# A smaller tile of zeros, a ninth product of zeros at the start, and one product fewer in two later waits

## The chip, the cores and the metric

The kernel runs on one core of a Trainium2 chip. The metric is the device time of one execution in microseconds (us). All executions told of here come from several chips, and each kernel is compared only with runs of the kernel before on the same chip, in the same rounds. One execution of each kernel was also traced by the hardware profiler; its span, from the first to the last instruction, is about 1.8 us shorter than its time.

## The reference, cut to what matters

Sliding-window attention with a linear bias (window 128) over 8 batches of 8 heads, 576 positions and 64 columns, followed by a gated feed-forward block on all 4608 tokens.

```python
scores = scale * np.matmul(q, k.transpose(0, 1, 3, 2))
...   # bias, mask to 128 positions back, softmax
x = attn_out.transpose(0, 2, 1, 3).reshape(B * S, H * D)      # 4608 x 512
g, val = x @ w_gate, x @ w_val                                # 512 -> 1536
return (gelu(g) * val) @ w_out                                # 1536 -> 512
```

## The kernel before

TensorE transposes the first batch's q and k, computes scores, sums, products of values and then the gate, value and output products of nine groups of 512 tokens. While it waits for the first loads, and in short waits after them, it multiplies zeros. `keep_busy(n)` puts n such products in front of the next use of a PSUM bank (the tile `ps` that a product writes).

```python
    def bank():
        ps = psum.tile([128, 512], FP32, name="ps")
        for _ in range(heat.pop()):
            nc.tensor.matmul(out=ps, lhsT=zeros[:, 0:128], rhs=zeros, start=True, stop=True)
        heat.append(0)
        return ps
    ...   # (cut)
    load_runs(0, 0, 0, 4)                       # first half of q and k, by GpSimd's queue
    zeros = consts.tile([128, 512], BF16, name="zeros")
    nc.vector.memset(zeros, 0.0)
    nc.vector.memset(ident, 0.0)
    ...   # (cut) second half of q and k, the rest of them, v, weights, in this order
    def first(cs):
        for w in (0, 1):                        # 0: q, 1: k
            if w and len(cs) == 2:
                keep_busy(3)
            for c in cs:
                ps = bank().bitcast(BF16)
                transpose_runs(0, 0, w, c, ps)
                untangle(dve, 0, 0, w, c, ps)   # copy by VectorE
    ...   # (cut)
    keep_busy(8)
    first((0, 1))
    made_later()
    keep_busy(4)
    scores(0, 0, (0, 1), lambda: (keep_busy(3), first((2,)), first((3,))))
```

I call the transposes of `first((2,))` and `first((3,))` the second halves.

The softmax here doesn't subtract the row's maximum and nothing guards it: scores larger than these inputs give would overflow.

Of the kernel before, what the change touches and what calls it, by code (L numbers as in the profile page):

```python
# [8 lines left out]
BF16 = mybir.dt.bfloat16  # L9
# [17 lines left out]
def kernel(  # L27
# [10 lines left out]
    nc = tc.nc  # L38
# [11 lines left out]
    consts = ctx.enter_context(tc.tile_pool(name="consts", bufs=1))  # L50
# [16 lines left out]
    def bank():  # L67
        ps = psum.tile([128, 512], FP32, name="ps")
        for _ in range(heat.pop()):
            nc.tensor.matmul(out=ps, lhsT=zeros[:, 0:128], rhs=zeros, start=True, stop=True)  # L70
        heat.append(0)
        return ps

    def keep_busy(n):
        heat[0] = n
# [36 lines left out]
    def runs(what, b, n):  # L112
        first, parts, r = RUNS[b][n]
        t, lo, p = (qs, ks)[what][b], 1536 * n, 0
        if (b, n) == (0, 1):

            t, lo = vb[1], 512 + 1024 * what
        elif b == 0:
            p = 64 * what
        return t.rearrange("p j x -> p (j x)")[p:p + parts, lo:lo + 512 * r].rearrange(  # L120
            "p (h x) -> p h x", h=H)

    def load_runs(b, n, h0, h1):
        first, parts, r = RUNS[b][n]
        for what, src in ((0, q), (1, k)):
            nc.gpsimd.dma_start(
                out=runs(what, b, n)[:, h0:h1, :],
                in_=src[b][h0:h1, first:first + parts * r, :].rearrange(
                    "h (p r) d -> p h (r d)", r=r))
# [14 lines left out]
    def transpose_runs(b, n, what, c, ps):  # L144

        first, parts, r = RUNS[b][n]
        src = runs(what, b, n)
        p = 64 * what if (b, n) == (0, 0) else 0
        for x in range(r):
            for i in (0, 1):  # L150
                nc.tensor.transpose(  # L151
                    out=ps[64 * i:64 * i + 64, parts * x:parts * x + parts],
                    in_=src[:, 2 * c + i, 64 * x:64 * x + 64],
                    identity=ident[p:p + parts, p:p + parts])

    def untangle(copy, b, n, what, c, ps):

        first, parts, r = RUNS[b][n]
        dst = by_pair((qT, kT)[what][b])[:, c, 64 + first:64 + first + parts * r]
        if isinstance(c, int):  # L160
            copy(out=dst.rearrange("p (x r) -> p x r", r=r),  # L161
                 in_=ps[:, 0:parts * r].rearrange("p (r x) -> p x r", r=r))
        else:
            n = c.stop - c.start
            copy(out=dst.rearrange("p c (x r) -> p c x r", r=r),
                 in_=ps[:, 0:n * parts * r].rearrange("p (c r x) -> p c x r", c=n, r=r))

    def transpose(b, what, c, copy):
        ps = bank().bitcast(BF16)
        for n, lo in ((0, 0), (1, 384)):  # L170
            transpose_runs(b, n, what, c, ps[:, lo:576])
        for n, lo in ((0, 0), (1, 384)):
            untangle(copy, b, n, what, c, ps[:, lo:576])
# [15 lines left out]
    def score(b, c, i, j, qj, n, ps, col):  # L189
        nc.tensor.matmul(  # L190
            out=ps[:, col:col + 128 * n].rearrange("p (n t) -> p n t", n=n),
            lhsT=blocks(kT, b, i, c, j, 1).rearrange("p n t -> p (n t)"),
            rhs=blocks(qT, b, i, c, qj, n),
            start=True, stop=True)

    def exp(dst, src):
        nc.scalar.activation(out=dst, in_=src, func=AF.Exp, scale=0.125)  # L197

    def mask(dst, m):
        nc.vector.tensor_tensor(out=dst, in0=dst, in1=m, op=ALU.mult)  # L200

    def scores2(b, later=None):

        P = p2_pool.tile([128, 4, 2, 128], BF16, name="P2")
        probs2[b] = P
        ps = [bank(), bank()]
        for c in range(4):
            for i in (0, 1):
                score(b, c, i, 2, 2, 1, ps[i], 128 * c)
        for i in (0, 1):  # L210
            exp(P[:, :, i, :], ps[i].rearrange("p (c n) -> p c n", c=4))
        if later is None:
            for i in (0, 1):
                mask(P[:, :, i, :], emask[:, i:8:2, 0:128])
        else:
            later.append((P.rearrange("p c i n -> p (c i) n"), emask[:, :, 0:128]))

    def scores(b, s, cs, then=None, later=None):


        pss = []
        for c in cs:
            ps = [bank(), bank()]
            pss.append(ps)
            for j, qj, n, col in (((0, 0, 2, 0), (1, 1, 2, 256)),
                                  ((4, 4, 1, 0), (2, 3, 1, 128), (3, 3, 2, 256)))[s]:
                for i in (0, 1):
                    score(b, c, i, j, qj, n, ps[i], col)
        if then:
            then()  # L230
        for c, ps in zip(cs, pss):
            P = p_pool[s].tile([128, 2, 512], BF16, name="P")
            probs[b, s, c] = P
            for i in (0, 1):
                exp(P[:, i, :], ps[i])
            args = (P.rearrange("p i (n x) -> p i n x", n=2),
                    emask[:, 2 * c:2 * c + 2, :].unsqueeze(2).to_broadcast((128, 2, 2, 256)))
            if later is None:
                mask(*args)
            else:  # L240
                later.append(args)
# [182 lines left out]
    def out_last(g):  # L424
# [10 lines left out]
                              in_=osb[:, 0:256])  # L435


    load_runs(0, 0, 0, 4)
    zeros = consts.tile([128, 512], BF16, name="zeros")
    nc.vector.memset(zeros, 0.0)  # L440
    nc.vector.memset(ident, 0.0)
    nc.gpsimd.affine_select(
        out=ident, in_=ident, compare_op=ALU.not_equal, fill=1.0,
# [6 lines left out]
    for half, base, step, chan in ((0, 0, 1, -1), (1, -1, -1, 1)):  # L450
        t = tmpl[:, 128 * half:128 * half + 128]
        nc.gpsimd.affine_select(
            out=t, in_=t, compare_op=ALU.is_ge, fill=1e9,
# [46 lines left out]
    def first(cs):  # L500
        for w in (0, 1):
            if w and len(cs) == 2:
                keep_busy(3)
            for c in cs:
                ps = bank().bitcast(BF16)
                transpose_runs(0, 0, w, c, ps)
                untangle(dve, 0, 0, w, c, ps)
# [5 lines left out]
                transpose_runs(0, 1, w, c, ps[:, 256 * k:256 * k + 256])  # L513
            untangle(act, 0, 1, w, slice(cs[0], cs[-1] + 1), ps)

    keep_busy(8)
    first((0, 1))
    made_later()
    keep_busy(4)
    scores(0, 0, (0, 1), lambda: (keep_busy(3), first((2,)), first((3,))))  # L520
    keep_busy(2)
    scores(0, 0, (2, 3))
    scores2(0)
# [27 lines left out]
    for n in range(2):  # L551
        nc.gpsimd.dma_start(
            out=wo[:, 6 * n:6 * n + 6, :],
# [114 lines left out]
```

## Time and profile before

| | kernel before |
|---|---|
| time, 3 runs | 357.66, 357.76, 359.34 us |
| span in the trace | 355.6 us |
| TensorE busy | 98% of the span |
| products of zeros | 25, all before 13.2 us |
| first product, first gate product | 1.20 us, 18.70 us |

TensorE sets the time. So the question is how early the dense gate products can begin: in the traces below, the span is the start of the first gate product's weight load plus 336.9 to 337.0 us in all traces but one (337.5). The views are shown in the prediction.

### The profile page before, as it was taken

Reading aid. Unit: us, or ns where it says so; the run is one execution under the profiler, and the core shown is the slowest. Engines: PE = TensorE matmul, PEld = TensorE weight load, DVE = VectorE, ACT = ScalarE, POOL = GpSimd, SP = SyncE. Lnnn points to the kernel's source line nnn. Section 1 sums busy time; section 2 is a strip of 40 time slices with the busy share of each in tenths; the row PEclk is TensorE's granted clock in tenths of the full one; section 3 lists DMA queues with packets and bytes.
Section 4 is the critical chain, followed back from the end, with each engine's and each line's share of the span. In section 5 each row is a group of like instructions: output and inputs, shape, how many; then the busy total and the mean of one; then the engine's idle time right before and its main releaser. Section 6 shows DMA issues by size and latency. Waiting matters only on the chain.

```text
span 355.6 us, 7101 instructions
## 1 busy us (share of the span) xinstructions
PE 348.9 (98%) x2869; PEld 174.6 (49%) x2869; DVE 188.3 (53%) x327; ACT 185.8 (52%) x342; POOL 103.1 (29%) x137
## 2 busy tenths in 40 slices
PE   8999999999999999999999999999999999999996
PEld 3667545444454445445444545454444444444443
DVE  4876578344988646646455554655474404403320
ACT  5884495536877375633873297337832233313322
POOL 8943479500940275003900192004000000000000
PEclk9999999999999999999999999999999999999999
DMA  7999999999999099983997399859206020011002
GB/s 93 182 195 197 202 160 193 148 154 166 141 157 174 12 185 180 158 177 41 153 208 151 78 133 200 142 129 98 88 4 133 32 88 1 2 68 50 2 29 88
DMA packets 145632, 42.62 MB, mean 120 GB/s; under 512 B 131608, under 2 KB 138520, under 8 KB 145600
## 3 DMA queue, kind: packets, MB, share of 16 engines
q0 software_dynamic: 106368, 18.88, 69.5%
q1 hardware_dynamic: 36432, 17.31, 22.2%
q10 hardware_dynamic: 2800, 5.99, 7.8%
q8 instruction: 22, 0.36, 0.4%
q14 instruction: 10, 0.08, 0.1%
HBM read 43.65 MB, written 9.53 MB: 150 GB/s over the span
## 4 chain that ended last, share of the span: by engine, by line
PE 94%; DVE 4%; issue 0%; ACT 0%; ACTq 0%; DVEq 0%
PE ps L392 53%; PE ps L415 25%; PE ps L358 5%; PE ps L190 4%; PE ps L70 2%; PE ps L315 2%; DVE P L200 1%; DVE r L321 1%; PE ps L151 1%; PE ps L429 1%; DVE kT L161 1%; PE ps L295 1%; PE ps L282 0%; PE ps L341 0%; DVE xT L379 0%
## 5 line engine op out<-in xcount | busy, mean ns | idle before, releaser
L399 DVE TENSOR_TENSOR hT<-ps,gelu 128x512 bf16<-128x512 f32 (+2 forms) x115 | 73.7, 653 | 105.8 <-PE ps L392 90.8
L398 ACT ACTIVATE gelu<-ps 128x512 bf16<-128x512 f32 (+2 forms) x115 | 65.1, 571 | 115.3 <-PE ps L392 111.5
L392 PE MATMUL ps<-xT,wg 128*128 128x512 bf16 (+2 forms) x460 | 112.3, 367 | 0.2
L392 PE MATMUL ps<-xT,wv 128*128 128x512 bf16 (+2 forms) x460 | 112.1, 366 | 0.0
L415 PE MATMUL ps<-wo,hT 128*128 128x512 bf16 x420 | 95.7, 380 | 0.0
L197 ACT ACTIVATE P<-ps 128x512 bf16<-128x512 f32 x144 | 73.1, 631 | 7.0 <-PE ps L190 7.0
L392 PEld LDWEIGHTS <-wv 128*128 128x128 bf16 x460 | 44.6, 98 | 48.8
L392 PEld LDWEIGHTS <-wg 128*128 128x128 bf16 x460 | 43.2, 98 | 47.4 <-issue 0.5
L200 DVE TENSOR_TENSOR P<-P,emask 128x1024 bf16<-128x1024 bf16 (+1 forms) x79 | 49.1, 641 | 30.1 <-ACT P L197 29.7
L415 PEld LDWEIGHTS <-hT 128*128 128x128 bf16 x420 | 38.9, 98 | 47.9 <-issue 3.7
L99 POOL DMA_DIRECT2D vb<-in_v_dram x40 | 33.9, 887 | 13.0 <-DMA ks<-in_k_dram 6.5
L420 ACT COPY osb<-ps 128x512 f32<-128x512 f32 x31 | 18.6, 601 | 32.8 <-PE ps L415 32.8
L621 POOL COPY mark<-hT 1x2 bf16<-1x2 bf16 x4 | 0.7, 174 | 95.0 <-DVE hT L399 95.0
L368 DVE TENSOR_TENSOR xT<-ps,rb 128x256 bf16<-128x256 f32 (+1 forms) x60 | 22.9, 443 | 9.2 <-DMA rb<-rd 4.7
L321 DVE RECIPROCAL r<-ps 128x320 f32<-128x320 f32 (+1 forms) x14 | 26.6, 1931 | 1.3 <-PE ps L315 1.3
L99 POOL DMA_DIRECT2D qs<-in_q_dram x30 | 25.2, 862 | 7.2 <-DMA wo<-in_moe_w_out_dram 5.1
L99 POOL DMA_DIRECT2D ks<-in_k_dram x30 | 25.4, 899 | 2.8 <-DMA qs<-in_q_dram 2.6
L190 PE MATMUL ps<-qT,kT 64*128 64x256 bf16 (+1 forms) x384 | 22.3, 244 | 1.4 <-DVE kT L161 0.6
L190 PEld LDWEIGHTS <-kT 64*128 64x128 bf16 x384 | 13.4, 94 | 13.6 <-issue 9.5
L358 PE MATMUL ps<-P,vb 128*64 128x128 bf16 (+2 forms) x384 | 18.1, 244 | 0.0
L358 PEld LDWEIGHTS <-vb 128*64 128x64 bf16 x384 | 14.7, 110 | 5.2 <-issue 4.8
L70 PE MATMUL ps<-zeros 128*128 128x512 bf16 x25 | 8.3, 460 | 1.2 <-DVE zeros L440 1.2
(73 smaller groups left out, 117.4 us busy)
## 6 DMA issues: line engine op xcount, KB each, us to landing
out_dram<-osb SPq DMA_DIRECT2D x35, 256.0 KB, 3.9
rb<-rd ACTq DMA_DIRECT2D x10, 576.0 KB, 7.4
vb<-in_v_dram POOLq DMA_DIRECT2D x32, 128.0 KB, 7.3
qs<-in_q_dram POOLq DMA_DIRECT2D x24, 128.0 KB, 6.2
ks<-in_k_dram POOLq DMA_DIRECT2D x24, 128.0 KB, 6.6
wo<-in_moe_w_out_dram POOLq DMA_DIRECT2D x2, 768.0 KB, 18.3
wg<-in_moe_w_gate_dram POOLq DMA_DIRECT2D x2, 384.0 KB, 9.2
wv<-in_moe_w_val_dram POOLq DMA_DIRECT2D x2, 384.0 KB, 10.7
```

The source lines that it names most:

```text
L99: nc.gpsimd.dma_start(out=t[lo:128, j, :].rearrange("p (h d) -> p h d", h=H), in_=src[b][:, 128 * j - 64 + lo:128 * j + 64, :].rearrange(" ...
L190: nc.tensor.matmul(out=ps[:, col:col + 128 * n].rearrange("p (n t) -> p n t", n=n), lhsT=blocks(kT, b, i, c, j, 1).rearrange("p n t -> p ( ...
L197: nc.scalar.activation(out=dst, in_=src, func=AF.Exp, scale=0.125)
L200: nc.vector.tensor_tensor(out=dst, in0=dst, in1=m, op=ALU.mult)
L321: nc.vector.reciprocal(row(b)[:, lo:hi], ps[:, 0:hi - lo])
L358: nc.tensor.matmul(out=ps[64 * i:64 * i + 64, a:e], lhsT=vb[b % 2][:, j, 64 * h:64 * h + 64], rhs=prob(b, s, c, i, j, e - a), start=(j == ...
L368: nc.vector.tensor_tensor(out=xT[:, c, b * S + lo:b * S + hi], in0=ps[:, 0:hi - lo], in1=recip[b][:, c, lo:hi], op=ALU.mult)
L392: nc.tensor.matmul(out=ps[:, 0:hi - lo], lhsT=w[:, c, 128 * f:128 * (f + 1)], rhs=xT[:, c, t0 + lo:t0 + hi], start=(c == 0), stop=(c == 3))
L398: nc.scalar.activation(out=gl[:, 0:hi - lo], in_=pg[:, 0:hi - lo], func=AF.Gelu)
L399: nc.vector.tensor_tensor(out=hid[g][:, f, lo:hi], in0=pv[:, 0:hi - lo], in1=gl[:, 0:hi - lo], op=ALU.mult)
L415: nc.tensor.matmul(out=po, lhsT=hid[g][:, f, 128 * t:128 * (t + 1)], rhs=wo[:, f, :], start=(f == 0), stop=(f == NF - 1))
L420: (nc.vector.tensor_copy if g < 2 and t < 2 else nc.scalar.copy)(out=osb, in_=po)
```

## The change

It is meant to start the products of zeros sooner, so that TensorE's clock rises sooner, and to spend less on them once the clock is up (in the trace of the kernel before, one takes 0.427 us at half rate and 0.215 at full). The diff, whole but for context lines:

```diff
-            nc.tensor.matmul(out=ps, lhsT=zeros[:, 0:128], rhs=zeros, start=True, stop=True)
+            nc.tensor.matmul(out=ps.rearrange("p (n x) -> p n x", n=4), lhsT=zeros,
+                             rhs=zeros.unsqueeze(1).to_broadcast((128, 4, 128)),
+                             start=True, stop=True)
@@
+    zeros = consts.tile([128, 128], BF16, name="zeros")
+    nc.vector.memset(zeros, 0.0)
     load_runs(0, 0, 0, 4)
-    zeros = consts.tile([128, 512], BF16, name="zeros")
-    nc.vector.memset(zeros, 0.0)
@@
             if w and len(cs) == 2:
-                keep_busy(3)
+                keep_busy(2)
@@
-    keep_busy(8)
+    keep_busy(9)
@@
-    scores(0, 0, (0, 1), lambda: (keep_busy(3), first((2,)), first((3,))))
+    scores(0, 0, (0, 1), lambda: (keep_busy(2), first((2,)), first((3,))))
```

## The prediction

> **What bounds the kernel now.** I first read the page of the profile: one core, its span, busy shares and the chain that ended last.
>
> ```profile
> span 355.6 us, 7101 instructions
> ...
> PE 348.9 (98%) x2869; PEld 174.6 (49%) x2869; DVE 188.3 (53%) x327; ACT 185.8 (52%) x342; POOL 103.1 (29%) x137
> ...
> PE 94%; DVE 4%; issue 0%; ACT 0%; ACTq 0%; DVEq 0%
> ...
> L70 PE MATMUL ps<-zeros 128*128 128x512 bf16 x25 | 8.3, 460 | 1.2 <-DVE zeros L440 1.2
> ```
>
> TensorE is busy 98% of the span and holds 94% of the chain. The change touches only the last line: 25 products of zeros, which compute nothing. All of them lie in the first 13 us, so the most that could be at stake is the 1.2 us before the first and their 8.3 us, 9.5 of 357.8 us or 2.7%, and the change removes one product net. What matters is whether that one, and the order of the rest, is on the path. For this I read the timeline of the first 16 us, in which several rows of one kind are merged (start, length, what, count, idle before).
>
> ```profile
> 0.87 0.27 DVE L440 MEMSET zeros<- 128x256 uint32 x1 [0.87 <-PEq L652]
> 1.11 0.11 DVE L441 MEMSET ident<- 128x64 uint32 x1
> ...
> 1.20 3.55 PE L70 MATMUL ps<-zeros 128*128 128x512 bf16 x8 [1.20 <-DVE zeros L440]
> ...
> 2.46 0.15 PEld L70 LDWEIGHTS <-zeros 128*128 128x128 bf16 x1 [0.28 <-issue]
> ...
> 2.88 0.15 PEld L70 LDWEIGHTS <-zeros 128*128 128x128 bf16 x1 [0.28 <-issue]
> ...
> 4.68 0.39 PEld L151 LDWEIGHTS <-qs 64*64 64x64 bf16 x20 [0.79 <-DMA qs<-in_q_dram]
> ...
> 5.11 0.82 PE L70 MATMUL ps<-zeros 128*128 128x512 bf16 x3
> ...
> 5.86 0.39 PEld L151 LDWEIGHTS <-ks 64*64 64x64 bf16 x20 [0.42 <-DMA ks<-in_k_dram]
> ...
> 7.81 0.82 PE L70 MATMUL ps<-zeros 128*128 128x512 bf16 x3
> ```
>
> Two things are to be seen. The first eight products step by 0.427 us (2.46 to 2.88), the later three by 0.215 us ((0.82 - 0.39 of one) / 2): TensorE doubles its rate between. The trace's record of the granted clock puts the step to full at 4.57 us of the span. Second, the idle times said to end with a DMA are not quite that. The last of eight starts at 1.20 + 7 x 0.427 = 4.19 by this step (4.16 in a narrow window of the timeline) and has streamed at 4.59; the transposes start at 4.68, 0.09 later. The last of three starts at 5.55, has streamed at 5.77, and the next transposes start at 5.86, again 0.09 later. The loads are in by then: issue at 1.25 plus 3.3 us to landing is 4.55 for q, 1.99 + 3.5 is 5.49 for k. So the transposes of k have waited for a product of zeros, by some 0.3 us, not for the load; those of q have waited for both about equally. The second waits are alike: the half loads land at 3.92 + 3.3 = 7.2 and 4.54 + 3.5 = 8.04, while the transposes start at 8.56.
>
> Last, the chain of the first 20 us shows what follows them.
>
> ```profile
> 7.88 0.75 PE ps L70 x3
> 8.63 0.29 PE ps L151 x14
> 8.93 0.02 issue
> 8.95 0.49 DVE qT L161
> 9.44 0.40 DVE kT L161
> 9.84 0.40 DVE qT L161
> 10.24 0.41 DVE kT L161
> 10.65 0.05 issue
> 10.69 0.62 PE ps L190 x12
> ```
>
> The products at 7.8, the transposes, four copies on VectorE and the next scores form one chain. What ends earlier at 7.8 ends earlier at 10.7.
>
> [...]from the first product to the step it is 4.57 - 1.20 = 3.37 us. [...]No product with such a repeated operand is in this trace. [...]The trace has 0.27 us for 256 elements and 0.11 for 64, so 0.16 us less for a quarter of the tile.
>
> **The change part by part.** The smaller tile takes the time of ident's equal memset, 0.11 for 0.27: the first product starts at 1.20 - 0.16 = 1.04. Moving it ahead of the load in the program moves nothing in time: the load is GpSimd's, the memset is already VectorE's first work.
>
> The ninth product starts at 1.04 + 8 x 0.427 = 4.45. If the clock steps up at 4.57 as before, 0.12 us of it is done at half rate (144 of 512 columns); the other 368 columns take 0.215 x 368/512 = 0.15, and it has streamed at 4.73. With the 0.09 gap, q's transposes start at 4.82, 0.14 later than 4.68. If the clock rises 3.37 us after the first product, at 4.41, the ninth is at full rate and q's transposes start near 4.75, 0.07 later. If the clock is still half at the end of nine, 0.27 later.
>
> Two instead of three before the transposes of k: 0.215 less at full rate, so they start 0.07 earlier in the middle case (0.14 earlier, 0.06 later in the others). The load at 5.49 allows it. Two instead of three before the second halves: again 0.215 less, so 0.29 earlier in the middle case (0.36 and 0.16): 8.56 becomes 8.27, still behind the landing at 8.04.
>
> This passes through the four copies to the scores at 10.69. What could stop it later is a load. The second run of k is issued at 6.03 and lands 6.0 us later, at 12.03; its transposes are the second half of the sixteen at 12.21, so needed near 12.40: 0.37 us of slack for the 0.29. Weights come next. The first value weights are issued at 10.05 and the gate product on them runs at 19.24; those issued at 11.52 land 9.3 us later, at 20.8, and are first used at 21.42: 0.6 us of slack. From there TensorE is dense. The waits of TensorE for the whole span name no DMA, so I let the saving through to the end. Sum: between 0.16 and 0.36 us, 0.25 us as my working figure, 0.07% of 357.76.
>
> **The rivals.** First, the step of the clock as a lottery. Before's three times are 357.66, 359.34 and 357.76. [...]the measured excess is 359.34 - 357.66 = 1.68. [...]the median of runs that are mostly early gains nothing.[...]
>
> Second, the ninth product may simply delay q's transposes with the clock still low, and the loads of the second halves (8.04) or of k's second run (12.03) may stop what the later two save. Each has only 0.2 to 0.4 us of slack, and landings move by some tenths. Then nothing is gained: 357.7 to 357.8.
>
> [...]
>
> Fourth, the repeated operand could be slower, say by a tenth. Twenty-four products then cost some 0.5 us at most, and 357.8 to 358.
>
> **Range and chances.** The middle is 357.76 - 0.25 = 357.5. The low end takes the larger saving and a lucky spread of the runs, 357.0. The high end has to hold a median that the late step has partly caught, 358.7. The 2% limits are 7.2 us away[...], and no saving that large is there at all: within 2% is nearly sure.
>
> **What would show it.** The zeros memset at 0.11 us; the first product near 1.04; nine with a 0.427 step, the ninth perhaps shorter; q's transposes near 4.8; k's near 5.8; the second halves near 8.3; the scores now at 10.69 near 10.4, and the first gate product now at 18.70 near 18.4. I am wrong in the mechanism if q's transposes start at 4.68 or sooner, if k's start at 5.86 with the DMA as true releaser, or if the gate product starts no earlier although 10.4 was met: then a load took over. A clock that steps up past 5 us in the profiled run would show the lottery. A time under 357.0 or over 358.7 in most runs would mean that the clock's step, not the count of products, decides.

The sum came to 0.25 us saved (0.16 to 0.36). That the repeated operand keeps the step of 0.427 us was an assumption.

## The result, and the profile after

| | before | after |
|---|---|---|
| median, 6 runs each | 358.23 us | 357.73 us |
| range | 357.66 to 359.34 us | 357.29 to 359.18 us |
| span in the trace | 355.6 us | 355.5 us |

The ratio is 0.9988, with a 95% interval of 0.9964 to 1.0012: the same within noise. Here and below, a ratio is the one for the runs of the two kernels in the same rounds; it isn't quite the ratio of the medians or of the plain means.

The page of the kernel after, the lines that answer to those shown of before:

```profile
span 355.5 us, 7099 instructions
...
PE 348.9 (98%) x2868; PEld 174.6 (49%) x2868; DVE 188.1 (53%) x327; ACT 185.9 (52%) x342; POOL 103.4 (29%) x137
```

These differ from before by 0.3 us or less, and by one product and its weight load. The difference is in the first 20 us. The timeline of the kernel after (start, length, engine, line, what, count, idle before; line numbers are two higher than in the kernel before):

```profile
0.83 0.11 DVE L441 MEMSET zeros<- 128x64 uint32 x1 [0.83 <-PEq L654]
...
1.00 3.63 PE L70 MATMUL ps<-zeros 128*128 128x512 bf16 x9 [1.00 <-DVE zeros L441]
...
4.71 0.39 PEld L153 LDWEIGHTS <-qs 64*64 64x64 bf16 x20 [0.59 <-DMA qs<-in_q_dram]
...
5.68 0.39 PEld L153 LDWEIGHTS <-ks 64*64 64x64 bf16 x20 [0.42 <-DMA ks<-in_k_dram]
...
8.16 0.17 PEld L153 LDWEIGHTS <-qs 64*64 64x64 bf16 x6 [0.42 <-issue]
...
14.54 0.78 PEld L360 LDWEIGHTS <-vb 128*64 128x64 bf16 x20 [0.26 <-DMA vb<-in_v_dram]
```

The memset takes 0.11 us and the first product starts at 1.00. Nine products take 3.63 us, only 0.08 more than eight did, because the record of the granted clock has its step to full at 4.12 us here, 0.45 us sooner than in the trace of before. The transposes of q then wait for q itself (4.67), those of k start 0.18 us sooner than in the kernel before (5.86), the second halves 0.40 us sooner (8.56). The chain confirms that this reaches the scores:

```profile
7.70 0.54 PE ps L70 x2
8.23 0.29 PE ps L153 x15
...
9.84 0.41 DVE kT L163
...
10.29 0.61 PE ps L192 x12
```

The scores of before ran at 10.69, so 0.40 us is still there at 10.29. Then it is taken back in two places. The first is the last line of the timeline above: the products of values, at 14.15 instead of 14.55, stop before the 14.54 row for the third block of v. It landed at 14.50; in the trace of before it landed at 14.23, was first needed at 14.66, and nobody waited. The first gate product is at 18.50, 0.20 us sooner than 18.70. The second place is the third gate group, whose value weights landed at 21.25. The weight loads and products there, first of the kernel before and then of the kernel after:

```profile
21.28 0.51 PEld L392 LDWEIGHTS <-wv 128*128 128x128 bf16 x4
...
21.42 0.71 PE L392 MATMUL ps<-xT,wv 128*128 128x320 bf16 x4
```

```profile
21.29 0.39 PEld L394 LDWEIGHTS <-wv 128*128 128x128 bf16 x4 [0.25 <-DMA wv<-in_moe_w_val_dram]
...
21.30 0.72 PE L394 MATMUL ps<-xT,wv 128*128 128x320 bf16 x4
```

The weight loads start at the same time in both, but in the kernel before they run ahead of a product at 21.42, and in the kernel after they have waited for the data and the product follows at once, at 21.30. From there to the end the two traces run 0.1 us apart. Of 0.40 us saved, 0.1 us is left.

That accounts for the two traces, not for the half microsecond between the two medians. Both kernels' times are spread over 1.7 to 1.9 us, and each traced execution (357.38 and 357.29 us) was at the fast end of its kernel's. The experiments had to say what makes that spread.

### The profile page after: what moved, and what is told of

Same layout as the page of the kernel before. It is cut to its first block, busy times and chain, and to the rows that moved or that the text cites. A ratio compares the mean times of both kernels' runs of the same rounds, so it can differ in the third digit from the quotient of the medians.

```text
span 355.5 us, 7099 instructions
## 1 busy us (share of the span) xinstructions
PE 348.9 (98%) x2868; PEld 174.6 (49%) x2868; DVE 188.1 (53%) x327; ACT 185.9 (52%) x342; POOL 103.4 (29%) x137
## 4 chain that ended last, share of the span: by engine, by line
PE 93%; DVE 4%; DMA 1%; issue 1%; ACT 0%; ACTq 0%; DVEq 0%; POOLq 0%
PE ps L394 53%; PE ps L417 25%; PE ps L360 5%; PE ps L192 4%; PE ps L317 2%; DVE P L202 1%; DVE r L323 1%; PE ps L153 1%; DMA qs<-in_q_dram 1%; PE ps L70 1%; PE ps L431 1%; DVE kT L163 1%; PE ps L297 1%; PE ps L284 0%; PE ps L343 0%
```

## The experiments

The theory was: removed products save up to 0.4 us, and loads take most of it back. The rivals: the sooner start is what gains (A), or the moment of the clock's step decides (B). Twelve experiments ran, all with correct outputs. "Step" is the first time at full clock in the trace's record of the granted clock; landing times are the last of a load's semaphore updates.

### 1. The two later waits alone

```diff
 (kernel before)
-                keep_busy(3)
+                keep_busy(2)
-    scores(0, 0, (0, 1), lambda: (keep_busy(3), first((2,)), first((3,))))
+    scores(0, 0, (0, 1), lambda: (keep_busy(2), first((2,)), first((3,))))
```

> The kernel before with only the two later waits cut from three products to two; the start (eight products, large tile) is untouched. Theory (the saving comes from the two removed products and the loads then cap it): the second halves' transposes start about 0.43 us earlier than in the kernel before (8.56 to near 8.13) once the clock is up, the first gate product (18.70) comes 0.2 to 0.3 us earlier, and after the gate products near 21 us only 0.1 to 0.2 us are left; ratio 0.9993 to 0.9998. Rival A (the sooner start is what gains): nothing earlier at 8.56, ratio 1.000. Rival B (the clock's step decides): the profiles differ by when the products of zeros change from 0.427 to 0.215 us apart, and the timed runs scatter by over 1 us whatever the count.

In the trace the step is at 4.48, the second halves start at 8.09 (0.47 sooner than before), the third block of v lands at 14.64, and the span is 355.5. The chain that ended last in the first 24 us runs through that load:

```profile
8.59 6.05 DMA vb<-in_v_dram
14.64 0.04 issue
14.69 0.99 PE ps L358 x20
```

The first gate product's weight load is at 18.62, only 0.05 us sooner than in the kernel before. So two fewer products do save what was reckoned, and the loads take it back: the theory's picture. But the six times are 357.25, 357.33, 357.75, 358.00, 360.32 and 360.35, ratio 1.0003 (0.9973 to 1.0033). The run of 360.32 had a mean granted clock of 0.995, which is 1.8 us lost at most (0.5% of its span of 358.5); the other, of 360.35, had 1.000. The mean leaves out the half rate before the step (it is 0.999 in the trace of experiment 3, whose step came at 8.11), so it says nothing of a late one. And it counts the fall of the clock after TensorE's last product if that lies within the span (0.998 in the trace of experiment 4; in that of before the last product ends at 352.06, the record falls to half at 356.15, past the end of the span, and the mean is 1.000). So a fall of the clock can't be what the two have in common.

### 2. The sooner start alone

```diff
 (kernel after)
-                keep_busy(2)
+                keep_busy(3)
-    scores(0, 0, (0, 1), lambda: (keep_busy(2), first((2,)), first((3,))))
+    scores(0, 0, (0, 1), lambda: (keep_busy(3), first((2,)), first((3,))))
```

> The changed kernel with three products again in the two later waits: the sooner start, the small tile and the ninth product alone. Theory: q's transposes as in the changed kernel (4.7 to 4.85), k's at 5.9, second halves at 8.5 to 8.6, no lasting gain: span within 0.1 us of the kernel before, ratio 1.000. Rival A (the sooner start gains): second halves at 8.2 and the whole gain kept. Rival B (fewer late steps of the clock): the timed runs lie closer together than those of the kernel before, none over 358.5.

The times are 357.52 to 358.30, ratio 0.9986 (0.9972 to 0.9999), under 1 by a hair; none is over 358.3, as rival B said. The trace has a later step. It is at 5.20, all nine products run at half rate, and q's transposes start at 4.95, as in the third case of the prediction. The chain:

```profile
1.00 4.02 PE ps L70 x9
...
5.54 0.75 PE ps L70 x3
...
8.24 0.75 PE ps L70 x3
8.99 0.29 PE ps L153 x14
...
11.05 0.62 PE ps L192 x12
```

The span is 356.5, a full 1.0 us more than in the trace of the kernel after. The later step is not all of that: the second halves start 0.76 us later, and 0.43 of this are the two products put back, 0.33 the step. The sums after them (L284, for the softmax) take 1.30 us instead of 0.89, because of a stop that is told of below.

### 3. No products at the start

```diff
 (kernel after)
-    keep_busy(9)
+    keep_busy(0)
```

> The changed kernel without the nine first products; TensorE begins with q's transposes. Both theories expect these near 4.65 at half rate[...]. If the cold work is on the path it costs half of the time until the step, [...]less what the loads hide: time 358.3 to 360, ratio 1.002 to 1.006. If the clock hardly matters here (rival: loads hide it): under 0.3 us, ratio 1.000 to 1.001.

Times 358.55 to 360.37, ratio 1.0038 (1.0020 to 1.0057). This is the one clear difference of all: without the products at the start the median is 1.2 us higher (359.71 against 358.52 for the kernel before in the same rounds). The step came at 8.11. TensorE's timeline in the cold:

```profile
4.46 0.74 PE L153 MATMUL ps<-ident,qs 64*64 64x64 bf16 x20 [4.46 <-DMA qs<-in_q_dram]
5.14 1.04 PE L70 MATMUL ps<-zeros 128*128 128x512 bf16 x2
6.10 0.74 PE L153 MATMUL ps<-ident,ks 64*64 64x64 bf16 x20
6.78 1.68 PE L70 MATMUL ps<-zeros 128*128 128x512 bf16 x4
```

Twenty transposes take 0.74 us against 0.50 at full rate, two products 1.04 against 0.61, four 1.68 (the last partly at full rate) against 1.04. So work before the step lies on the path.

### 4. No products in the two later waits

```diff
 (kernel after)
-                keep_busy(2)
+                keep_busy(0)
-    scores(0, 0, (0, 1), lambda: (keep_busy(2), first((2,)), first((3,))))
+    scores(0, 0, (0, 1), lambda: (keep_busy(0), first((2,)), first((3,))))
```

> The changed kernel with no products at all in the two later waits (nine at the start stay). Theory (loads cap): k's transposes move to its landing (about 5.5), the second halves' to the landing of k's second half (about 8.05 to 8.1), the scores now at 10.29 to about 10.1, and nothing of it is left at the gate products near 21 us: span within 0.1 us of the changed kernel. Rival (products count one for one): four fewer products give 0.86 us less, span 354.7. Rival (the clock falls or steps later with fewer products): products after 8 us 0.427 apart, 1 us or more lost.

Times 357.46 to 358.12, ratio 0.9983 (0.9970 to 0.9997). In the trace the step is at 6.62, and the second halves start at 7.79, sooner than in any other kernel. The first gate product's weight load is at 19.37 all the same, later than in the kernel after (18.48): the second block of v landed at 14.64 and the third at 15.39. The rival that counts products one for one (span 354.7) is out: the span is 356.3, and no run took less than 357.46. That the second halves beat the landing of k's second half (7.93) by starting with q was not foreseen. The intervals of experiments 2 and 4 end just under 1, although their traces are slower than the kernel before's; the runs of the kernel before that both share had drawn a median of 358.52, against 358.05 and 358.04 in the two calls that followed, but 358.54 in the last one. So that draw was not an unusual one, and a gain of some 0.15% in these two kernels stays possible. Two of thirteen intervals that just miss 1 don't show it, and neither kernel was run again.

### A stop that is neither clock nor load of data

Three of the four traces (experiments 2, 3 and 4) stop for another 0.14 to 0.29 us in a place that the kernels before and after pass without a stop. "Issue" is time in which the engine waited for nothing that the profile shows. The same place in a repeat of the kernel after (5, below):

```profile
8.60 0.29 PE ps L153 x14
...
10.65 0.62 PE ps L192 x12
...
13.69 0.70 PE ps L284 x24
14.39 0.54 issue
14.93 0.34 PE ps L284 x8
```

The sums (L284) stop for 0.54 us. I counted TensorE's recorded instructions (weight loads, products, two of its sequencer) before such stops. It is 449, in each of the traces that stop there by more than 0.2 us, though the kernels have different numbers of instructions in front: the stop falls after 61, 63, 64 or 67 of the 72 sums. The page's instruction queue moves 22 packets of 16 KB; one such packet ends between 10.6 and 14.4 us in each trace. In nine traces the stop (0.06 to 1.04 us) ends 1.35 to 1.53 us after that packet's end. In the kernels before and after it was in by 12.60 and 12.45, 1.65 and 1.40 us ahead of the 450th instruction, and nothing stopped. (In experiment 1 it was in 1.27 us ahead without a stop; records of products are missing there.) I read this as TensorE waiting for its own instructions; that is a reading of these times, and no run proves it. What makes the packet late is not shown: the packet itself takes 0.94 to 1.07 us in all 14 traces, and no run varied only what else the DMA engines carried. The queues' view of the kernel after from 11 to 12 us and of the repeat from 12 to 13 us (packets, MB, share):

```profile
q8 instruction: 1, 0.02, 6.1%
```

```profile
q8 instruction: 1, 0.02, 6.5%
```

The sums of the kernel after, for comparison, ran in one piece:

```profile
13.33 0.89 PE ps L284 x31
```

In the repeat they take 1.58 us from first to last, 0.69 more: the stop of 0.54, and 0.15 that the sums on its two sides take more.

### 5. The kernel after, again

No edit.

> The changed kernel once more[...]. [...]the step falls at another time than 4.12 us[...]; a step past 5 us puts the second halves' transposes past 8.3[...]. Timed runs spread from 357.2 to about 358.7, median near 357.8. If instead the step follows the first product by a fixed time (rival), it is 4.1 again and the runs lie within 0.3 us apart from the loads.

The step is at 5.29, not 4.12, so it doesn't follow the first product by a fixed time: 4.29 us after it here, 3.12 there. Times 358.03 to 359.07, ratio 1.0009 (0.9996 to 1.0022); span 356.2. With experiment 2 this makes a pair whose steps lie 0.09 us apart, three products against two: second halves 8.92 and 8.53, first gate load 19.60 and 19.32, spans 356.5 and 356.2. At a like step the two removed products are worth about 0.4 us early and 0.3 us at the end, as far as one pair of traces can say.

### 6. The two later waits alone, again

No edit to experiment 1.

> The kernel before with two products in the later waits once more, because two of its six timed runs took 360.3 and one of these had a mean granted clock of 0.995. [...]one or two of six runs are over 359.5 again. If that was chance, all are under 359.3, as the kernel before's.

Times 357.54 to 358.82, ratio 1.0004 (0.9990 to 1.0018): no run near 360. Whether two of eleven runs at 360.3 belong to this kernel or to chance stays open; no trace fell on one. This trace has a step at 5.05, a stop of 0.91 us before the 450th instruction, and the slowest span of the kernels without new loads, 357.0.

### 7. The loads eased

```diff
 (kernel after)
-    load_w(256, 640)
+    load_w(256, 384)
+    load_w(384, 640)
 (first products of values: loop over blocks of keys outside, pairs of heads inside)
```

> The changed kernel with its two load waits eased: the first products of values run by block of keys, so that the third block of v is needed about 0.7 us later, and the weights of columns 256 to 640 come in two pieces, so that the third gate group needs only the first. If the loads took back the saving, the first gate product comes 0.2 us earlier than in the changed kernel for the same step of the clock (18.5 to near 18.3), no wait for wv near 21.2, and the span is 355.2 to 355.3 where the clock steps before 4.6; time 0.2 to 0.3 us less. Rival: the extra pieces slow all loads and nothing is gained, or another load takes over.

Inconclusive. The step came at 6.79 and the instructions late (13.97, a stop of 0.40 us), so that TensorE was behind its loads anyway: first gate load 19.81, span 356.8. Times 357.43 to 358.56, ratio 1.0002.

### 8 and 12. The start on a constant

```diff
 (kernel after)
-    zeros = consts.tile([128, 128], BF16, name="zeros")
-    nc.vector.memset(zeros, 0.0)
+    zeros = nc.const_aps.tensor(1.0, (128, 128), BF16)
```

> The changed kernel with its products on the constant 1.0[...], one element read 128 and 512 times, in place of the tile of zeros: no memset is waited for. The first product starts near 0.75, not 1.00. If a sooner start makes the late step of the clock rarer, the median falls by about 0.1 us and the slowest run lies under 358.5[...]. Rival (start doesn't matter): same as the changed kernel. It could be slower if a product of ones or of a repeated element runs at another rate: then its 0.427 step differs.

> The start on the constant once more, because its median of 357.44 was the lowest of all runs and five runs are few. If the first product at 0.73 instead of 1.00 makes a step of the clock before 4.6 us more frequent, the median is again under 357.8 and the ratio to the kernel before under 0.9990. If the first five were a lucky draw[...], the median is 357.9 to 358.4 and the ratio 0.9995 to 1.0005, as the changed kernel's repeats.

The first product is at 0.79 in both. The steps are at 5.13 and 6.67, the spans 356.8 and 356.2. First times 357.24 to 358.58, median 357.44, ratio 0.9990 (0.9976 to 1.0005); then 357.70 to 358.27, median 358.00, ratio 0.9991 (0.9969 to 1.0013). The second median is over the 357.8 that I had asked for, the ratio is between my two cases. A gain of a tenth of a per cent may be there; these runs don't show it.

### 9. The first products in quarters

```diff
 (kernel after, the nine first products only)
+            for x in range(4 * n):
+                lo = 128 * (x % 4)
+                nc.tensor.matmul(out=ps[:, lo:lo + 128], lhsT=zeros, rhs=zeros,
+                                 start=True, stop=True)
```

> The changed kernel with its nine first products each cut into four of 128 columns: the same columns, 54 more TensorE instructions (27 loads of weights and 27 products). In six traces so far TensorE stood still for 0.25 to 1.04 us before exactly its 450th recorded instruction, whatever the kernel, 1.35 to 1.54 us after a block of instructions (16 KB, the page's instruction queue) had arrived late, at 13.4 to 14.4. If that block is the cause, [...]the standstill before the first products of values is gone or moved to the sums and under 0.3 us; median 0.1 to 0.4 us under the changed kernel's of the same call. Rival: the standstill belongs to the loads of v; then it stays before the last sums or first products. Rival: [...]the clock steps later; then the 0.427 step per 512 columns lasts past 7 us.

This tests the instruction block. It arrived at 12.71, and although the step was the latest of all kernels with products at the start (7.01), the stop is gone. The chain has the sums in one piece:

```profile
14.40 0.89 PE ps L291 x31
```

First gate load 19.33 and span 356.2, against 19.81 and 356.8 in experiment 7 with its step at 6.79. But that quarters bring the block in sooner was the assumption, and 12.71 doesn't show it: without quarters it came by 12.60 in the traces of before, after and experiment 1, and experiment 12, with its step at 6.67, stopped for only 0.06 us and has the same span of 356.2. So this trace agrees with the block as the cause of the stop, but doesn't show that quarters brought it in sooner: that may be the draw. The median, 357.99, hardly moves: ratio 0.9995 (0.9980 to 1.0009), against 0.9996 of the kernel after.

### 10. All three

Quarters, constant and eased loads together.

> The quarters together with the start on the constant (first product near 0.75) and the eased loads. If the three causes found (late step of the clock, late block of instructions, loads of v and of the third gate group) are the ones, it is the fastest: median 357.1 to 357.3, slowest under 358.3, ratio to the kernel before 0.997. Rival: some other load takes over and it is no faster than the changed kernel, 357.7 to 358.

Times 357.89 to 358.84, ratio 1.0003 (0.9988 to 1.0018): the combination isn't faster. Its trace has an early step (4.19), the second halves at 8.12, the instruction block as early as 10.63 and no stop for it, and yet a span of 357.1. The weight loads for the rest of k show why:

```profile
13.32 0.25 PEld L160 LDWEIGHTS <-vb 128*64 128x64 bf16 x8 [1.10 <-DMA vb<-in_k_dram]
```

This load landed at 13.28, over a microsecond later than in the kernels before and after (12.03 and 11.97). A further 0.38 us went to a wait for value weights near 28.4. Another load took over, as the rival said. That the early instruction packet delayed the data is possible, but no run shows it.

### 11. The kernel after

No edit.

> The changed kernel again, for a comparison in the same rounds: median 357.6 to 358.1, from 357.2 to 359; the trace draws another step of the clock; if the step falls after 4.8 and the block of instructions arrives after 12.6, a standstill before the 450th instruction shows, as in r1.

Times 357.26 to 358.57, ratio 0.9996 (0.9979 to 1.0013). Step 5.82, instructions in at 13.99, stop 0.86 us, span 356.8, as expected for such a draw.

### The traces side by side

| kernel | first product | step | second halves | block of instructions in | stop | first gate load | span |
|---|---|---|---|---|---|---|---|
| before | 1.20 | 4.57 | 8.56 | 12.60 | none | 18.67 | 355.6 |
| after | 1.00 | 4.12 | 8.16 | 12.45 | none | 18.48 | 355.5 |
| after, 5 | 1.00 | 5.29 | 8.53 | 13.51 | 0.53 | 19.32 | 356.2 |
| after, 11 | 1.00 | 5.82 | 8.72 | 13.99 | 0.86 | 19.85 | 356.8 |
| two later, 1 | 1.20 | 4.48 | 8.09 | 12.59 | none | 18.62 | 355.5 |
| two later, 6 | 1.21 | 5.05 | 8.30 | 14.39 | 0.91 | 20.12 | 357.0 |
| quarters, 9 | 1.00 | 7.01 | 9.23 | 12.71 | none | 19.33 | 356.2 |

One kernel differs from itself by 1.3 us (after) and 1.5 us (two later) between traces, three to five times what the change can save (0.3 to 0.4 us). Late steps and late instruction blocks come together in most of these, but not one for one (the last two rows).

For the kernel after, the three traces can be reckoned through. In the repeats the first gate product comes 0.85 and 1.37 us later than in the first trace. The second halves, moved by the step, are 0.37 and 0.56 later; the sums take 0.69 and 1.02 longer, because of the stop; and the wait for the third block of v, 0.21 us in the first trace, falls away. That adds up to 0.85 and 1.37. So the stop is the larger part of what the traced executions of this one kernel differ by, and the step of the clock the smaller. Whether a late step also makes the block of instructions late, no run separates.

## Why the prediction was right

**The number.** 357.5 was predicted with a range of 357.0 to 358.7; the median is 357.73, and the repeats' medians, 358.20 and 358.36, lie in the range too. The changed kernel has a median of 358.04 in 17 runs and the kernel before 358.26 in 48, on several chips. The three ratios are 0.9988, 1.0009 and 0.9996, and each interval holds 1. A saving of 0.25 us, 0.07%, is compatible with them and not shown by them.

**The start.** Right: memset 0.11 us, first product 1.00 (1.04 predicted), the 0.427 step kept with the repeated operand. Of the three cases for the ninth product, an early step (0.07 later, predicted start 4.75; measured 4.71, by the landing of q) and a late one (0.27 later; measured 4.95) were both drawn.

**The two later waits.** Right in mechanism: k's transposes had waited for a product of zeros, and they moved. 0.29 us was the working figure at the second halves; 0.40 was measured in the traced pair, since the step came sooner, and 0.39 in the pair of experiments 2 and 5.

**The step that failed** is "so I let the saving through to the end". It rested on slacks of 0.37 us and 0.6 us taken from one trace. It never reckoned the slack of the third block of v, 0.43 us by that trace (14.66 less 14.23), and after the scores this was the load that stopped TensorE first. Landings move by more than that: the rest of k from 11.73 to 13.28, the third block of v from 13.84 to 15.74. In the traced pair the loads took 0.3 of 0.4 us. The term of the sum is the end of the chain: 0.1 us in place of 0.25. The sentence that no wait of TensorE names a DMA was true of the products in a trace that had drawn early landings (the weight loads' own list names the first loads of q and k). The second rival, that loads stop what is saved, was the nearer to it, though with v and the third gate group rather than the loads it named.

**The clock's step.** It was rightly named as a lottery, but the odds were wrong: "the median of runs that are mostly early gains nothing". The 3.37 us from TensorE's first work to the step in the trace of before was one draw: over the traces it is 3.12 to 6.01 us. A step by 4.6 us came in only 4 of the 14 traces. The trace of before, the fastest of its first runs, had looked like the normal case. Early and late steps differ by up to 1.1 us at the second halves (8.16 and 9.23, both with two products in the waits), and this, with the loads and the stop before the 450th instruction, makes the spread of the traced spans; the untraced times can't be taken apart like this. That the run of 359.34 had one late step, as the prediction read it, stays unshown, and it didn't have the stop at all.

**The third and fourth rivals.** The repeated operand isn't slower (0.427 us at half rate, 0.215 at full, in the traces of before and after alike). (A tenth more on 24 products would have been about 0.7 us and not 0.5: nine at 0.427, fifteen at 0.215.) The mean granted clock stayed at 0.998 to 1.000 in the eleven times of no products in the waits (4) and of the repeat (6), so these show no fall by fewer products; the run with a clock of 0.995 in experiment 1 is the one sign that it may happen, and stays open.

## What to carry to other kernels

In the first microseconds of a kernel, a slack read from one trace is one draw: before you let a saving of a few tenths through, compare it with how far landings move between traces of the same kernel. A stop that the profile calls "issue" can be placed by counting instructions: here the stop near the sums came before the 450th in each trace where it was over 0.2 us, and it ended 1.35 to 1.53 us after the end of an instruction packet. That made the instructions the suspect, not the proven cause. And when a change is worth 0.1% and a kernel differs from itself by 0.4%, look at the span per trace and what each trace has drawn, because the medians can't tell one explanation from another.
